# A convolution by three triangle products in place of two, and a new order of the loop's work

## The chip, the cores and the metric

One core of a Trainium2 chip runs the whole program. The metric is the device time of one execution in microseconds, and lower is better. The kernel before was timed three times, and its median is the figure that the kernel after is compared with. One execution of it was also profiled; all rows in this document that are called rows of before come from that execution.

The engines are named here as in the profile. PE is TensorE, which multiplies matrices (PEld is its weight load). DVE is VectorE, ACT is ScalarE, POOL is GpSimd, and SP is the engine whose queue starts the DMA transfers. Each engine works through its own queue in order. An instruction that must wait holds up everything behind it on the same engine.

## The reference, cut to what matters

```python
x: (1, 2048, 448); 16 heads of 28; u is not used by the sum: the convolution is called with x
g = sigmoid((x * gate_w).sum(-1))
q, k, v = split(x @ wqkv)
phi(t) = where(t > 0, t + 1, exp(t)) + 1e-6
o = phi(q) (phi(k)^T v) / (phi(q) . sum(phi(k)) + 1e-6)   # per head, not causal
a = o @ wo
K[d, l] = 2 Re sum_n C[d, n] exp(A[d, n] dt[d] l)          # one filter of length 2048 per channel
b = causal_convolution(x, K) + x * D_skip
out = g * a + (1 - g) * b
```

The part that the change touches is the convolution. For the filters that these inputs have, the kernel writes the filter of each channel as a value (`near`) times a straight line in the lag with a small slope. Inside a chunk of 128 positions the convolution is then a product with a lower triangle of ones, applied to x and to x times the slope; what comes from earlier chunks is added later, from the last row of every chunk. A general path for other filters stands behind a test at the end of the program and is not taken here.

## The kernel before

**Tiles and chunks.** The 2048 positions are 16 chunks of 128, with the positions on the partitions. For each chunk `c` one load (line 229) brings x transposed in three and a half blocks (for the projections) and x itself, 1024 columns of float32 in all. Products are made in a reduced float32 format (`F32R`), and where full accuracy is wanted a number is split: a high part is cast to that format on ScalarE, and the low part is the difference.

- `split_x` (line 260) makes the high part of a chunk by one ScalarE cast of 1024 columns (line 272) and the two low parts by GpSimd subtractions (lines 273 and 274, both recorded at line 258, the helper `low`): one of 512 columns for the projections and one of 448 for x itself.
- `skip` (line 276) is the product of x with `D_skip`, on GpSimd.

**The loop over c from 1 to 14** (line 520) is software-pipelined over several chunks. One iteration makes

- the k projection of chunk `c+1`: eleven matmuls into the one PSUM buffer "k" (line 534, recorded at 370), and on it the feature map: two exponentials on ScalarE (lines 396 and 397), add and max on VectorE (line 398), the high part on ScalarE (line 402), and the low part and the running sum `zb` on VectorE (both recorded at 408);
- the q projection of chunk `c`: eleven matmuls into the one buffer "q", then the gate's and the feature's exponentials on ScalarE (lines 416 and 385) and two VectorE operations (lines 386 and 389);
- eleven matmuls that add x's outer product with k to four accumulators (`do_g`, line 431, recorded at 438);
- one or two chunks of the convolution. It starts with a lag, from c=4 on (`LAG` is 3), and the iterations in `TWICE` (4, 5, 6, 8, 10, 12) take two chunks, so that the 16 chunks are done at c=13.

**One chunk of the convolution.** `do_wa` (line 449, recorded at 451) multiplies the high part of x by `slope` on VectorE; `do_wb` (line 453, recorded at 455) subtracts that from the low part, also on VectorE. `do_v` (line 457) adds two matmuls with the triangle `tri`: over the high part and over this difference. Its PSUM buffers "v0" and "v1" alternate. `v_post` (line 462, recorded at 464) multiplies the result by `near` on VectorE and sends its last row to `u` by a small DMA on SP's queue; `v_add` (line 469, recorded at 470) adds it to `y`, with both inputs in SBUF.

**The order.** The tile framework is used with a manual schedule: every engine runs its instructions in the order in which the program writes them, and what a reader sees in the loop body is the order of each queue. In an iteration the program writes the k projection, w of the next convolution chunk (up to c=11), `v_post` of the last one, the cast and the low parts of x of chunk `c+2` and its skip product, `v_add`, then the whole k feature, and in an iteration of `TWICE` the second convolution chunk with its `v_post` and `v_add`; then the q projection with its feature, more of w, the outer products, and the convolution matmuls of the next chunk. At c=4 the cast of chunk 6 comes later, since its buffer is still held by chunk 0 (six buffers for split chunks, three for loaded ones). At c=11 and 13 the output weight `wo` is split as well: a ScalarE cast of 896 columns (line 550) and a GpSimd subtraction (line 554). Small steps that prepare `slope` and `near` (`s4d_prepare`, line 305) are spread over the first iterations by `steps`.

**Behind the loop** come the all-reduce of `zb` over the partitions by an all-ones product, the gate, the normalisers of q (`norm_a` to `norm_d`), the block products with v and wo, and a last stage (`attend`, line 676) that makes eleven matmuls per chunk and writes the output.

Of the kernel before, what the change touches and what calls it, by code (L numbers as in the profile page):

```python
# [7 lines left out]
F32 = mybir.dt.float32  # L8
# [7 lines left out]
P = 128  # L16
# [15 lines left out]
QA = (2, 2, 5)  # L32
TWICE = (4, 5, 6, 8, 10, 12)
SMALL = 2.0 ** -70
# [137 lines left out]
def gated_mix_kernel(ctx: ExitStack, tc: tile.TileContext, xin, wk_d, wq_d, wv_d, wo_d, abc_d, ldt_d, dsk_d,  # L172
# [84 lines left out]
    def low(eng, o, r, h):  # L257
        eng.tensor_tensor(out=o, in0=r, in1=h.bitcast(F32), op=ALU.subtract)  # L258

    def split_x(c):  # L260
        r = xr[c]
        w = xs.tile([P, XW], F32R, name="xw", tag="x")
        h, l = xh[c], xl[c] = w, w[:, LT:]
        if c < 2:
            ACT.copy(h[:, :NAT], r[:, :NAT])
            if c == 0:
                ACT.copy(wkh[:, 0], wkr[:, 0])
            low(DVE, l, r[:, :NAT], h[:, :NAT])
            if c == 0:
                low(DVE, wkh[64:, 0], wkr[64:, 0], wkh[64:, 0])  # L270
        else:
            ACT.copy(h[:, :XC], r)  # L272
            low(POOL, l, r[:, :NAT], h[:, :NAT])
            low(POOL, h[:, XC:LT], r[:, NAT:LO], h[:, NAT:LO])

# [105 lines left out]

    def feature(dst, o, mid=None):
        e = tp.tile([P, D], F32, name="e", tag="e")
        t = tp.tile([P, D], F32, name="t", tag="t")
        ACT.activation(e, o[:, :D], AF.Exp)  # L385
        DVE.tensor_scalar(out=t, in0=e, scalar1=1.0, scalar2=1e-6, op0=ALU.min, op1=ALU.add)  # L386
        if mid:
            mid()
        DVE.scalar_tensor_tensor(out=dst, in0=o[:, :D], scalar=C1, in1=t, op0=ALU.add, op1=ALU.max)  # L389
# [10 lines left out]
    def k_high(c):  # L400
        pkh[c] = tp.tile([P, D], F32R, name="pkh", tag="pkh")
        ACT.add(pkh[c], pks[c], 1e-6)  # L402

    def k_low(c):
        pk = pks.pop(c)
        pkl[c] = tp.tile([P, D], F32R, name="pkl", tag="pkl")
        for o, a, op in ((pkl[c], pkh[c].bitcast(F32), ALU.subtract), (zb, zb, ALU.add)):
            DVE.scalar_tensor_tensor(out=o, in0=pk, scalar=1e-6, in1=a, op0=ALU.add, op1=op)  # L408

    def k_post(c, o):  # L410
        k_feature(c, o)
        k_high(c)
        k_low(c)

    def q_post(c, o, mid=None):
        ACT.activation(e1[:, c:c + 1], o[:, D:D + 1], AF.Exp, scale=-1.0)
        feature(pq[:, c], o, mid)

# [23 lines left out]

    def do_w(c, eng):
        do_wa(c)
        do_wb(c, eng)

    wq = {}

    def do_wa(c):
        q = wq[c] = tp.tile([P, D], F32, name="q", tag="t")  # L450
        DVE.tensor_tensor(out=q, in0=xh[c][:, NAT:LO].bitcast(F32), in1=slope, op=ALU.mult)  # L451

    def do_wb(c, eng):
        w = wt[c] = tp.tile([P, D], F32R, name="w", tag="w")
        eng.tensor_tensor(out=w, in0=xh[c][:, XC:LT].bitcast(F32), in1=wq.pop(c), op=ALU.subtract)  # L455

    def do_v(c):
        v = vt[c] = ps.tile([P, 512], F32, name="v", tag="v%d" % (c % 2))
        PE.matmul(v[:, :D], lhsT=tri, rhs=xh[c][:, NAT:LO], start=True, stop=False)
        PE.matmul(v[:, :D], lhsT=tri, rhs=wt.pop(c), start=False, stop=True)  # L460

# [42 lines left out]
    k_feature(1, ko)  # L504
    split_rest(0)
    k_low(0)
    skip(0)
# [3 lines left out]
    q_post(0, qo)  # L511
    split_x(2)
    k_low(1)
    skip(1)
# [5 lines left out]
    for c in range(1, NC - 1):  # L520
# [13 lines left out]
        ko = project(c + 1, wkh, wkl, D, "k")  # L534
        if c > LAG and c < 12 and vs[c in TWICE:]:
            do_w(vs[c in TWICE], DVE)
        if vq:
            v_post(vq[0])
        if c == NC - 2:
            zr = z_products()  # L540
            pick = xs.tile([P, 5, P], F32R, name="pick", tag="x")[:DJ]
            ACT.copy(pick, pickr)
        if c + 2 < NC and c != LAG + 1:
            split_x(c + 2)
            skip(c + 2)
        if c in (NC - 5, NC - 3):
# [3 lines left out]
            ACT.copy(woh[-1], wo[:, 2 * len(woh) - 2:2 * len(woh)])  # L550
        if vq:
            v_add(vq.pop(0))
        if c in (NC - 5, NC - 3):
            low(POOL, wol[-1], wo[:, 2 * len(wol) - 2:2 * len(wol)], woh[-1])
        if c > LAG and c >= 12 and vs[c in TWICE:]:
            do_w(vs[c in TWICE], DVE)
        k_post(c + 1, ko)
        if c == NC - 2:
# [3 lines left out]
            low(DVE, zl, zb, zh)  # L562
        if c in TWICE:
            v_next()
            v_post(vq[0])
            if c > LAG + 1:
                v_add(vq.pop(0))
        if c == LAG + 1:
            split_x(c + 2)
            v_add(vq.pop(0))  # L570
            skip(c + 2)
        if c == 1:
            steps(1)
        if c > 1:
            qo = project(c, wqh, wql, D + 2, "q")
            if c == LAG:
                do_g(c, (0,))
                steps(1)
                do_wa(vs[0])
                q_post(c, qo, lambda: do_wb(vs[0], DVE))  # L580
                steps(1)
            else:
                q_post(c, qo)
        if c == 2:
            steps(1)
        if c + 1 in TWICE and c > LAG:
            do_w(vs[c > LAG], DVE)
        if c < NC - 2:
            do_g(c, range(c == LAG, 4))
        if c == LAG:  # L590
# [377 lines left out]
```

## Time and profile before

| | us |
|---|---|
| median of three runs (211.17 to 213.93) | 212.77 |
| the profiled execution | 211.4 |
| its span, from the first to the last instruction | 209.6 |
| TensorE busy, 895 matmuls | 179.2 |
| VectorE busy, 298 instructions | 169.4 |
| GpSimd busy, 106 instructions | 105.7 |
| ScalarE busy, 192 instructions | 94.6 |

A row of a timeline gives the start and the duration in microseconds, the engine, the line of the kernel, the operation, what is written and read with its shape, and how many equal instructions follow one another in it. Brackets at the end hold the idle time ahead of it and what ended it. A row of the groups has the total busy time and the mean of one instruction in nanoseconds behind the bar, then the idle time ahead of them. A row of a line has the shortest, the middle and the longest duration. A row of the chain has start, duration and what it was. Matmuls overlap: one of 448 columns is listed with some 360 ns, while the next one starts earlier than that.

### The profile page before, as it was taken

The numbers are of one execution on the slowest core, as the hardware profiler recorded it, in microseconds if no ns is written. First come the engines' busy times: TensorE is split into PE (matmuls) and PEld (weight loads), VectorE is DVE, ScalarE is ACT, GpSimd is POOL, SyncE is SP. The second block draws the span as 40 slices with busy tenths as digits, with TensorE's granted clock in tenths as the row PEclk, the third lists the DMA queues.
The fourth block names the chain that finished last, engine by engine and source line by source line (L and its number), as shares of the span: only waits on it lengthen the run. The fifth ranks groups of instructions, "written<-read, shape, count | busy, mean of one in ns | idle before, by whom it ended". The sixth has DMA issues, their size and how long they took to land.

```text
span 209.6 us, 2815 instructions
## 1 busy us (share of the span) xinstructions
PE 179.2 (85%) x895; PEld 155.3 (74%) x895; DVE 169.4 (81%) x298; ACT 94.6 (45%) x192; POOL 105.7 (50%) x106
## 2 busy tenths in 40 slices
PE   7889699996986798969869596798979999999990
PEld 6678599895866687758748495695858989999980
DVE  2586479889998989898899889868979979998540
ACT  5695883354041442323260543336157456555530
POOL 1079959019560708254365619213655886886000
PEclk9999999999699999999999999999999999999997
DMA  5997946503020220033020302000000122222221
GB/s 199 338 296 250 276 135 246 184 2 104 0 85 16 100 79 21 0 105 100 0 97 5 105 0 55 5 15 0 4 2 0 44 93 90 89 89 90 91 110 36
DMA packets 8198, 18.65 MB, mean 89 GB/s; under 512 B 1756, under 2 KB 5040, under 8 KB 7952
## 3 DMA queue, kind: packets, MB, share of 16 engines
q1 hardware_dynamic: 8176, 18.39, 26.6%
q8 instruction: 9, 0.15, 0.3%
q14 instruction: 13, 0.11, 0.2%
HBM read 14.54 MB, written 3.67 MB: 87 GB/s over the span
## 4 chain that ended last, share of the span: by engine, by line
DVE 47%; PE 29%; issue 7%; ACT 7%; DMA 4%; POOL 2%; SPq 1%; DVEq 0%; ACTq 0%; POOLq 0%
PE a L686 17%; DVE y L470 8%; DVE q L451 6%; DVE w L455 5%; PE k L370 4%; DVE t L386 4%; DVE t L464 4%; DVE k L398 4%; DVE zb L408 4%; ACT pkh L402 3%; DVE pq L389 3%; PE tr L664 3%; DVE pkl L408 2%; DMA y<-in 2%; DMA xr<-in 2%
## 5 line engine op out<-in xcount | busy, mean ns | idle before, releaser
L258 POOL TENSOR_TENSOR xw<-xr,xw 128x448 fp32r<-128x448 f32 (+1 forms) x30 | 40.8, 1381 | 52.6 <-ACT xw L272 21.1
L370 PE MATMUL q<-wqh,xw 128*128 128x450 f32 x120 | 33.7, 383 | 6.8 <-DVE pq L389 4.8
L370 PE MATMUL k<-wkh,xw 128*128 128x448 f32 x120 | 32.7, 374 | 6.8 <-DVE zb L408 5.8
L438 PE MATMUL g<-pkh,xw 128*128 128x448 f32 x112 | 35.8, 367 | 0.0
L370 PEld LDWEIGHTS q<-wqh,xw 128*128 128x128 f32 x120 | 23.1, 196 | 10.6 <-ACT e L397 7.5
L370 PEld LDWEIGHTS k<-wkh,xw 128*128 128x128 f32 x120 | 21.6, 188 | 12.0 <-ACT e L385 4.0
L402 ACT ACTIVATE pkh<-k 128x448 fp32r<-128x448 f32 x15 | 8.2, 544 | 42.3 <-DVE k L398 42.3
L686 PE MATMUL a<-wkh,th 128*128 128x448 f32 (+1 forms) x119 | 26.9, 365 | 0.0
L603 POOL TENSOR_TENSOR prod<-pq,zb 128x448 f32<-128x448 f32 x16 | 18.5, 1161 | 10.4 <-ACT zb L709 6.1
L438 PE MATMUL g<-pkl,xw 128*128 128x448 f32 x64 | 23.6, 369 | 0.0
L438 PEld LDWEIGHTS g<-pkh,xw 128*128 128x128 f32 x112 | 21.0, 188 | 2.6
L686 PEld LDWEIGHTS a<-wkh,th 128*128 128x128 f32 x119 | 20.5, 189 | 1.3
L396 ACT ACTIVATE e<-k 128x448 f32<-128x448 f32 x15 | 8.1, 543 | 29.3 <-PE k L370 29.3
L277 POOL TENSOR_TENSOR y<-xr,rows 128x448 f32<-128x448 f32 x16 | 20.7, 1297 | 0.0
L470 DVE TENSOR_TENSOR y<-y,t 128x448 f32<-128x448 f32 x16 | 16.8, 1049 | 0.6
L455 DVE TENSOR_TENSOR w<-xw,q 128x448 fp32r<-128x448 f32 x16 | 15.7, 982 | 1.5
L626 POOL TENSOR_TENSOR pn<-pq,den 128x336 f32<-128x336 f32 x16 | 12.1, 754 | 9.3 <-DVE den L615 5.2
L370 PE MATMUL q<-wql,xw 128*128 128x450 f32 x45 | 16.7, 378 | 0.0
L408 DVE SCALAR_TENSOR_TENSOR pkl<-k,pkh 128x448 fp32r<-128x448 f32 x15 | 9.4, 624 | 8.6 <-ACT pkh L402 8.6
L370 PE MATMUL k<-wkl,xw 128*128 128x448 f32 x45 | 16.2, 367 | 0.0
L272 ACT CAST xw<-xr 128x1024 fp32r<-128x1024 f32 x14 | 14.8, 1055 | 2.8 <-DMA xr<-in 1.5
L451 DVE TENSOR_TENSOR q<-xw,rows 128x448 f32<-128x448 f32 x16 | 15.4, 960 | 0.0
(163 smaller groups left out, 349.1 us busy)
## 6 DMA issues: line engine op xcount, KB each, us to landing
xr<-in SPq DMA_DIRECT2D x14, 512.0 KB, 4.3
out<-ot SPq DMA_DIRECT2D x15, 224.0 KB, 1.9
pq<-in SPq DMA_DIRECT2D x2, 896.0 KB
xr<-in SPq DMA_DIRECT2D x4, 256.0 KB
y<-in SPq DMA_DIRECT2D x2, 450.0 KB, 5.6
y<-in SPq DMA_DIRECT2D x4, 224.0 KB
wv<-in SPq DMA_DIRECT2D x1, 896.0 KB
wo<-in SPq DMA_DIRECT2D x1, 784.0 KB
```

Of the source, the lines that this page charges most:

```text
L258: eng.tensor_tensor(out=o, in0=r, in1=h.bitcast(F32), op=ALU.subtract)
L272: ACT.copy(h[:, :XC], r)
L277: POOL.tensor_tensor(out=y[:, c], in0=xr[c][:, NAT:LO], in1=dsk, op=ALU.mult)
L370: PE.matmul(o[:, :n], lhsT=a, rhs=b, start=run.n == 1, stop=not seq)
L402: ACT.add(pkh[c], pks[c], 1e-6)
L408: DVE.scalar_tensor_tensor(out=o, in0=pk, scalar=1e-6, in1=a, op0=ALU.add, op1=op)
L438: PE.matmul(g[i][:a.shape[1], :D], lhsT=a, rhs=b, start=c == 0 and n == 0, stop=c == NC - 1 and n == len(seq) - 1)
L451: DVE.tensor_tensor(out=q, in0=xh[c][:, NAT:LO].bitcast(F32), in1=slope, op=ALU.mult)
L455: eng.tensor_tensor(out=w, in0=xh[c][:, XC:LT].bitcast(F32), in1=wq.pop(c), op=ALU.subtract)
L470: DVE.tensor_tensor(out=y[:, c], in0=y[:, c], in1=vt.pop(c), op=ALU.add)
L603: POOL.tensor_tensor(out=pd[c], in0=pq[:, c], in1=zb, op=ALU.mult)
L686: PE.matmul(a[:, lo:hi], lhsT=u_, rhs=w_[:, lo:hi], start=n == 0, stop=n == 10)
```

## The change

Three things are changed.

1. The convolution of a chunk is made of three triangle products: over the high part of x, over its low part, and over minus the high part times `slope`. So w is one VectorE operation, a scalar_tensor_tensor with the scalar -1, and its subtraction from the low part is gone. There is one matmul more per chunk.
2. The order inside an iteration is another one. `v_post` and `v_add` come first, then w, then the k feature; only behind its two exponentials stands the cast of x, on GpSimd the low parts and the skip product behind it, and on ScalarE the high part of k. The low part and the running sum of k change places: the running sum is written ahead of the high part.
3. The second of the doubled iterations at the end is 13 in place of 12, the split of `wo` is written ahead of that of x, and the preparing steps at c=3 follow the q feature together.

```diff
-TWICE = (4, 5, 6, 8, 10, 12)
+TWICE = (4, 5, 6, 8, 10, 13)
...
+    def low_x(c):
+        r, h = xr[c], xh[c]
+        low(POOL, xl[c], r[:, :NAT], h[:, :NAT])
+        low(POOL, h[:, XC:LT], r[:, NAT:LO], h[:, NAT:LO])
+
...
             ACT.copy(h[:, :XC], r)
-            low(POOL, l, r[:, :NAT], h[:, :NAT])
-            low(POOL, h[:, XC:LT], r[:, NAT:LO], h[:, NAT:LO])
...
+    def k_sum(c):
+        DVE.scalar_tensor_tensor(out=zb, in0=pks[c], scalar=1e-6, in1=zb, op0=ALU.add, op1=ALU.add)
+
     def k_low(c):
-        pk = pks.pop(c)
         pkl[c] = tp.tile([P, D], F32R, name="pkl", tag="pkl")
-        for o, a, op in ((pkl[c], pkh[c].bitcast(F32), ALU.subtract), (zb, zb, ALU.add)):
-            DVE.scalar_tensor_tensor(out=o, in0=pk, scalar=1e-6, in1=a, op0=ALU.add, op1=op)
+        DVE.scalar_tensor_tensor(out=pkl[c], in0=pks.pop(c), scalar=1e-6, in1=pkh[c].bitcast(F32), op0=ALU.add,
+                                 op1=ALU.subtract)
...
-    def do_wa(c):
-        q = wq[c] = tp.tile([P, D], F32, name="q", tag="t")
-        DVE.tensor_tensor(out=q, in0=xh[c][:, NAT:LO].bitcast(F32), in1=slope, op=ALU.mult)
-
-    def do_wb(c, eng):
+    def do_w(c):
         w = wt[c] = tp.tile([P, D], F32R, name="w", tag="w")
-        eng.tensor_tensor(out=w, in0=xh[c][:, XC:LT].bitcast(F32), in1=wq.pop(c), op=ALU.subtract)
+        DVE.scalar_tensor_tensor(out=w, in0=xh[c][:, NAT:LO].bitcast(F32), scalar=-1.0, in1=slope, op0=ALU.mult,
+                                 op1=ALU.mult)
...
-        PE.matmul(v[:, :D], lhsT=tri, rhs=xh[c][:, NAT:LO], start=True, stop=False)
-        PE.matmul(v[:, :D], lhsT=tri, rhs=wt.pop(c), start=False, stop=True)
+        for n, w in enumerate((xh[c][:, NAT:LO], xh[c][:, XC:LT], wt.pop(c))):
+            PE.matmul(v[:, :D], lhsT=tri, rhs=w, start=n == 0, stop=n == 2)
...
         ko = project(c + 1, wkh, wkl, D, "k")
-        if c > LAG and c < 12 and vs[c in TWICE:]:
-            do_w(vs[c in TWICE], DVE)
         if vq:
             v_post(vq[0])
...
-        if c + 2 < NC and c != LAG + 1:
-            split_x(c + 2)
-            skip(c + 2)
+        if vq:
+            v_add(vq.pop(0))
         if c in (NC - 5, NC - 3):
             wos = xs.tile([DJ, 2, 2, D], F32R, name="wos", tag="x")
...
-        if vq:
-            v_add(vq.pop(0))
-        if c in (NC - 5, NC - 3):
             low(POOL, wol[-1], wo[:, 2 * len(wol) - 2:2 * len(wol)], woh[-1])
-        if c > LAG and c >= 12 and vs[c in TWICE:]:
-            do_w(vs[c in TWICE], DVE)
-        k_post(c + 1, ko)
+        if LAG < c < 13:
+            while vs and len(wt) < 1 + (c in TWICE):
+                do_w(vs[len(wt)])
+        k_feature(c + 1, ko)
+        if c + 2 < NC and c != LAG + 1:
+            split_x(c + 2)
+            low_x(c + 2)
+            skip(c + 2)
+        if (c == LAG + 1 or c in TWICE) and not wt:
+            do_w(vs[0])
+        if c == LAG + 1:
+            v_next()
+        k_sum(c + 1)
+        k_high(c + 1)
+        k_low(c + 1)
+        if c == LAG + 1:
+            split_x(c + 2)
+            low_x(c + 2)
+            skip(c + 2)
...
-        if c in TWICE:
+        if c == LAG + 1:
+            v_post(vq[0])
+            v_add(vq.pop(0))
+        elif c in TWICE:
             v_next()
             v_post(vq[0])
-            if c > LAG + 1:
-                v_add(vq.pop(0))
-        if c == LAG + 1:
-            split_x(c + 2)
             v_add(vq.pop(0))
-            skip(c + 2)
...
         if c > 1:
-            qo = project(c, wqh, wql, D + 2, "q")
+            q_post(c, project(c, wqh, wql, D + 2, "q"))
             if c == LAG:
-                do_g(c, (0,))
-                steps(1)
-                do_wa(vs[0])
-                q_post(c, qo, lambda: do_wb(vs[0], DVE))
-                steps(1)
-            else:
-                q_post(c, qo)
+                steps(2)
         if c == 2:
             steps(1)
-        if c + 1 in TWICE and c > LAG:
-            do_w(vs[c > LAG], DVE)
+        if c == LAG:
+            do_w(vs[0])
+        if c > LAG and vs and not wt:
+            do_w(vs[0])
         if c < NC - 2:
-            do_g(c, range(c == LAG, 4))
+            do_g(c)
```

More of the change, by code (lines that the diff above doesn't have):

```diff
@@ L380, in gated_mix_kernel, with feature @@
     C1 = 1.0 + 1e-6
-    def feature(dst, o, mid=None):
+    def feature(dst, o):
         e = tp.tile([P, D], F32, name="e", tag="e")
@@ L386, in feature @@
         DVE.tensor_scalar(out=t, in0=e, scalar1=1.0, scalar2=1e-6, op0=ALU.min, op1=ALU.add)
-        if mid:
-            mid()
         DVE.scalar_tensor_tensor(out=dst, in0=o[:, :D], scalar=C1, in1=t, op0=ALU.add, op1=ALU.max)
@@ L412, in k_post, with q_post @@
         k_high(c)
+        k_sum(c)
         k_low(c)
-    def q_post(c, o, mid=None):
+    def q_post(c, o):
         ACT.activation(e1[:, c:c + 1], o[:, D:D + 1], AF.Exp, scale=-1.0)
-        feature(pq[:, c], o, mid)
+        feature(pq[:, c], o)
     def do_q(c, tag="q"):
@@ L441, in gated_mix_kernel @@
     vt, wt = {}, {}
[L443 to L447, printed above, removed]
-    def do_wa(c):
-        q = wq[c] = tp.tile([P, D], F32, name="q", tag="t")
-        DVE.tensor_tensor(out=q, in0=xh[c][:, NAT:LO].bitcast(F32), in1=slope, op=ALU.mult)
-    def do_wb(c, eng):
+    def do_w(c):
         w = wt[c] = tp.tile([P, D], F32R, name="w", tag="w")
-        eng.tensor_tensor(out=w, in0=xh[c][:, XC:LT].bitcast(F32), in1=wq.pop(c), op=ALU.subtract)
+        DVE.scalar_tensor_tensor(out=w, in0=xh[c][:, NAT:LO].bitcast(F32), scalar=-1.0, in1=slope, op0=ALU.mult,
+                                 op1=ALU.mult)
     def do_v(c):
         v = vt[c] = ps.tile([P, 512], F32, name="v", tag="v%d" % (c % 2))
-        PE.matmul(v[:, :D], lhsT=tri, rhs=xh[c][:, NAT:LO], start=True, stop=False)
-        PE.matmul(v[:, :D], lhsT=tri, rhs=wt.pop(c), start=False, stop=True)
+        for n, w in enumerate((xh[c][:, NAT:LO], xh[c][:, XC:LT], wt.pop(c))):
+            PE.matmul(v[:, :D], lhsT=tri, rhs=w, start=n == 0, stop=n == 2)
     def v_post(c):
@@ L505, in gated_mix_kernel @@
     split_rest(0)
+    k_sum(0)
     k_low(0)
@@ L512, in gated_mix_kernel @@
     split_x(2)
+    low_x(2)
+    k_sum(1)
     k_low(1)
```

## The prediction

> **What bounds the kernel now.** I read the page first, for the budget and the chain that ended last.
>
> ```profile
> span 209.6 us, 2815 instructions
> PE 179.2 (85%) x895; PEld 155.3 (74%) x895; DVE 169.4 (81%) x298; ACT 94.6 (45%) x192; POOL 105.7 (50%) x106
> DVE 47%; PE 29%; issue 7%; ACT 7%; DMA 4%; POOL 2%; SPq 1%; DVEq 0%; ACTq 0%; POOLq 0%
> ```
>
> The chain is VectorE's for 47% of the span, though TensorE is the busier engine. Two engines take turns as the limit, so I cut the span into stages. After the window's bounds and length come busy times with counts: TensorE first, VectorE third, GpSimd fifth; then the granted clock.
>
> ```profile
> 43.01:138.62 95.61, 78.96 (x364) 67.61 (x363) 86.13 (x113) 33.36 (x63) 47.44 (x34) 0.98 0.15 48
> 50.70:57.00 6.30, 4.37 (x15) 3.92 (x15) 6.13 (x7) 1.02 (x2) 4.36 (x3) 0.73 0.01 4
> 161.35:204.00 42.65, 42.57 (x241) 38.56 (x240) 34.73 (x78) 22.42 (x51) 24.37 (x34) 1.00 0.22 83
> ```
>
> The first row is the loop from c=4 to c=14, between two starts of line 396, the first ScalarE operation on a k projection. There VectorE is busy 86.1 of 95.6 us. In the last row (attention) TensorE has no gap. Now a piece of the loop on VectorE, from c=8 into c=9:
>
> ```profile
> 88.27 1.52 DVE L470 TENSOR_TENSOR y<-y,t 128x448 f32<-128x448 f32 x1
> 89.71 1.33 DVE L386 TENSOR_SCALAR t<-e 128x448 f32<-128x448 f32 x1
> 91.14 0.62 DVE L389 SCALAR_TENSOR_TENSOR pq<-q,t 128x448 f32<-128x448 f32 x1
> 91.69 0.83 DVE L451 TENSOR_TENSOR q<-xw,rows 128x448 f32<-128x448 f32 x1
> ...
> 94.35 0.63 DVE L398 SCALAR_TENSOR_TENSOR k<-k,e 128x448 f32<-128x448 f32 x1
> ...
> 96.66 0.38 DVE L386 TENSOR_SCALAR t<-e 128x448 f32<-128x448 f32 x1
> ```
>
> The same operation has two durations: line 386 takes 1.33 and 0.38 us. What the other engines do meanwhile:
>
> ```profile
> 88.02 2.77 POOL L258 TENSOR_TENSOR xw<-xr,xw 128x512 fp32r<-128x512 f32 x2 [5.07 <-ACT xw L272]
> 90.75 1.28 POOL L277 TENSOR_TENSOR y<-xr,rows 128x448 f32<-128x448 f32 x1
> 90.97 0.58 ACT L397 ACTIVATE e<-e 128x448 f32<-128x448 f32 x1
> 95.02 0.55 ACT L402 ACTIVATE pkh<-k 128x448 fp32r<-128x448 f32 x1 [3.46 <-DVE k L398]
> 91.92 1.06 PE L370 MATMUL q<-wqh,xw 128*128 128x450 f32 x4 [1.61 <-DVE pq L389]
> ```
>
> The long ones fall into GpSimd's block of 88.02 to 92.03. Operations with a PSUM operand (389, 398) take 0.62 to 0.63 inside it and outside it. So an operation with two SBUF inputs, or the one-input line 386, waits for the GpSimd instruction that is running, and each GpSimd instruction can hold up one of them. The price of the queue is seen on ScalarE: the exponential of k was done at 91.55, VectorE came to line 398 at 94.35, and line 402 waited 3.46 us for that. TensorE's q projection waited 1.61 us for pq, line 389. The loop is bound by VectorE's in-order queue, lengthened by GpSimd.
>
> **The operand that goes.** Before, each of 16 chunks costs VectorE two operations; after, one.
>
> ```profile
> L451 DVE TENSOR_TENSOR q<-xw,rows x16: 612/828/1571, 40.2 to 132.3; 128x448 f32<-128x448 f32 x16
> L451 DVE TENSOR_TENSOR q<-xw,rows 128x448 f32<-128x448 f32 x16 | 15.4, 960 | 0.0
> L455 DVE TENSOR_TENSOR w<-xw,q 128x448 fp32r<-128x448 f32 x16 | 15.7, 982 | 1.5
> 26.66 0.69 DVE L317 SCALAR_TENSOR_TENSOR y<-pq 112x512 f32<-112x512 f32 x1
> 25.46 1.16 DVE L317 SCALAR_TENSOR_TENSOR y<-pq 112x512 f32<-112x512 f32 x1
> ```
>
> Removed: 15.4 + 15.7 = 31.1 us of VectorE. Added: 16 scalar_tensor_tensor on two SBUF inputs of 448. The nearest row is line 317, the same operation on 512: 0.69 us at best, so 0.6 for 448, and 1.16 in another instance. I take 0.6 where the order below puts it outside GpSimd's block (16 x 0.6 = 9.6 us, 21.5 less on VectorE); the upper end is 1.57, the longest of line 451 (25.1 us, 6.0 less). The Trainium skill, "SBUF — State Buffer", section "Who interferes with whom", says that a VectorE instruction with two SBUF inputs contends with a GpSimd instruction that reads SBUF, and that the loser blocks until the other is done. The trace agrees (0.61 to 1.57 for line 451); by that rule the new form escapes nothing, which is how I cost it.
>
> Added too: one more 448-column matmul per chunk.
>
> ```profile
> 28.19 2.26 PE q L370 x11
> ```
>
> 0.2055 us each, so 16 x 0.2055 = 3.3 us of TensorE: nothing where it waits anyway, all of it where it becomes the bound; 5.7 us at the 0.355 spacing of the slow stretch below.
>
> **The new order, in one iteration.** The undisturbed chain of a k projection is seen at c=14. The next two rows show GpSimd starting 1.14 us after the start of a cast of x, then a free pair of low parts, the casts' mean, and the split of wo on GpSimd.
>
> ```profile
> 138.37 0.98 PE L370 MATMUL q<-wqh,xw 128*128 128x450 f32 x4
> 138.62 0.55 ACT L396 ACTIVATE e<-k 128x448 f32<-128x448 f32 x1 [2.71 <-PE k L370]
> 139.81 0.63 DVE L398 SCALAR_TENSOR_TENSOR k<-k,e 128x448 f32<-128x448 f32 x1 [1.20 <-ACT e L397]
> 140.48 0.54 ACT L402 ACTIVATE pkh<-k 128x448 fp32r<-128x448 f32 x1 [0.70 <-DVE k L398]
> 141.06 0.62 DVE L408 SCALAR_TENSOR_TENSOR pkl<-k,pkh 128x448 fp32r<-128x448 f32 x1 [0.61 <-ACT pkh L402]
> 58.23 1.06 ACT L272 CAST xw<-xr 128x1024 fp32r<-128x1024 f32 x1
> 59.37 2.79 POOL L258 TENSOR_TENSOR xw<-xr,xw 128x512 fp32r<-128x512 f32 x2 [4.30 <-ACT xw L272]
> 22.60 2.38 POOL L258 TENSOR_TENSOR xw<-xr,xw 128x512 fp32r<-128x512 f32 x2
> L272 ACT CAST xw<-xr 128x1024 fp32r<-128x1024 f32 x14 | 14.8, 1055 | 2.8 <-DMA xr<-in 1.5
> L258 POOL TENSOR_TENSOR wos<-wo,wos 112x896 fp32r<-112x896 f32 x2 | 4.6, 2314 | 0.0
> ```
>
> Count from A, the start of line 396. TensorE passes from k to q at A-0.25. VectorE's add-max (398) starts at 1.19. The cast of x now stands behind the two exponentials (1.03 to 2.08), so line 402 starts at 2.08 instead of 1.86 and the low part (pkl) at 2.66; the running sum (k_sum) fills VectorE's idle 0.6 us before it. The move costs 0.22 us, hidden: k's PSUM buffer is free at 3.2, and TensorE wants it after q, g and v only, at 4.9. Were the cast held up by a late load, 1.7 us of cover are there. GpSimd's two low parts run from 2.17 to 4.5, the skip product to about 6.1 with what VectorE slips in between; TensorE wants the first low part at 4.9. The split of wo (2.3 us, c=11 and 13) moves ahead of the low parts, into GpSimd's idle time from 6.1 to the next A+2.17 (3.4 us); without it the low parts of x would come 2.3 us late, when TensorE wants them.
>
> An iteration with one v has 36 matmuls, 7.4 us; with two, 39, 8.0 us. VectorE in the 7.4: add-max 1.19, sum 1.73, pkl 2.66; line 386 blocked until the first low part ends at 3.4, done 3.8; pq 4.4; v_post 5.15 (v ends at 4.9); v_add blocked by the skip to 6.1, done 6.65; one or two w, 7.2 and 7.75; the next add-max is due at 7.4 + 1.19 = 8.6. It keeps up with 0.8 us to spare. In the 8.0: v_post at 3.2, v_add blocked to 4.5, line 386 by the skip to 6.25, pq done 7.2 (q's PSUM is wanted at 7.8), then v_post, v_add and w to 8.85, add-max due at 9.2: it keeps up too. TensorE waits only where w is late: the first v of an iteration with two wants w 0.16 us after A (two of its three matmuls need none).
>
> The sum, by c. 4: 8.0. 5: 9.0, as two such iterations follow one another and the w of chunk 2 comes 1.0 us late. 6 to 12: 8.0, 7.4, 8.0, 7.4, 8.0, 7.4, 7.4. 13: 8.0 and 2.6 of waits: chunk 14's w is made only after the add-max (done 2.3, wanted 0.16: 2.2 us), chunk 15's after pq (0.4 us). Together 81.2. Hand-overs take 0.04 (140.44 to 140.48) to 0.16 us (pq's end 91.76 to 91.92); one of 0.1 per iteration makes 82.3, against 95.6: -13.3 us.
>
> **Ahead of and behind the loop.**
>
> ```profile
> 25.70 1.05 PE L370 MATMUL k<-wkh,xw 128*128 128x448 f32 x4 [1.94 <-DVE zb L408]
> 142.25 0.57 ACT L561 CAST zh<-zb 128x448 fp32r<-128x448 f32 x1 [1.22 <-DVE zb L408]
> 144.91 1.01 DVE L425 TENSOR_SCALAR og<-og 128x15 f32<-128x15 f32 x1
> ```
>
> At c=2 the k projection waited 1.94 us for the sum, the second of two operations; now pkl is the last and done 0.5 to 0.7 us sooner, and the cast no longer stands ahead of the exponentials. Later casts move GpSimd's blocks too, which could take it back: -0.6, between 0 and -1.2. Behind c=14 the sum is ready at A+2.3; its cast ran at A+3.6 before. The all-ones product and the normalisers start some 0.7 us sooner, and the gate's small operations can get ahead of the GpSimd block that stretched line 425 to 1.01: -1.2, between -0.5 and -2.2.
>
> In all 13.3 + 0.6 + 1.2 = 15.1 us: span 194.5. The profiled execution lasted 211.4, 1.8 outside its span: 196.3. The median of the runs, 212.77, is 1.4 above that execution: **197.7 us**.
>
> **Rivals.** *The lock keeps VectorE the bound.* For it: three operations per iteration still meet GpSimd's three instructions, and GpSimd is busy in 47 of the 95.6 us. At worst two take 1.5 us and line 386 1.35: with three operations of the k chain (3 x 0.54 apart), v_post, pq (0.54 each) and 0.3 idle that is 7.35 with one v, hidden by 7.4; a second v adds v_post, v_add and w, 1.6 us free: 8.95 against 8.0. Six times 0.95 is 5.7 us: 203.4. Against it: w stands behind v_add, when GpSimd's block is over.
>
> *The cast waits, and the gain goes.* The cast now stands ahead of line 402 and q's exponentials on ScalarE; a late load delays k's PSUM. A wait of 3 us in each of ten iterations is 1.3 us beyond the cover, 13 us: 211. Against it: all casts together waited 1.5 us for loads, and the load issued in c=5 had ten microseconds before its cast at 58.23:
>
> ```profile
> 47.97 0.43 SPq L229 DMA_DIRECT2D xr<-in  x1
> ```
>
> *The slow clock, slower than before.*
>
> ```profile
> PE v L460 <- DVE w L455: 6.9, 5, 2.6
> 52.63 0.47 PE L460 MATMUL v<-w,tri 128*128 128x448 f32 x1 [1.93 <-DVE w L455]
> 56.54 0.36 PE L370 MATMUL q<-wql,xw 128*128 128x450 f32 x1
> ```
>
> After one of the five long waits for w the clock fell (0.73 in the window above): from 52.63, 11 matmuls came 0.355 us apart. 378 matmuls x 0.15 = 57 us if the whole loop ran so; from 34% of them (15.1 + 4.3 of 57) it is 2% slower: 217 and up, say 219. For it: waits of 1.0 and 2.2 us remain at c=5 and c=13. Against it: one fall in five waits, TensorE now idles less, and the gapless last 42.65 us ran at 1.00. The Trainium skill, "TensorE: Matmul & The Clock Gate", section "What's actually happening", says that idling throttles the clock and activity releases it, in windows of about 3.4 us; the trace's fall and recovery agree, and by that rule fewer waits mean fewer falls. One fall costs 11 x 0.15 = 1.6 us, which the range holds.
>
> **How the numbers follow.** TensorE as the loop's bound 0.66, own range 193.0 to 201.5 (below: 195.1 by the favourable ends, 81.2 + 1.2 + 2.2, and 2.1 of the 3.6 us of waits for w gone as well; above: one fall and 0.2 us more per iteration); the lock 0.22 (203.4); the late cast 0.08 (211); the slow clock 0.04 (219). 2% of 212.77, about what a measurement can tell from no change, is 4.3 us: faster means below 208.5. The first two are faster and a little of the third: 0.89; within 2% 0.07; slower 0.04. The range reaches over the lock's case: 193.0 to 204.5.
>
> **What would show it.** Right: 82 us between the starts of the first k exponential at c=4 and c=14, TensorE busy over 93% of them; v's third matmul waiting for w at c=5 and c=13 only; the k high part (402) waiting under 1 us for the add-max; the new w at 0.6 us; the running sum in VectorE's former idle time. Wrong: w at 1.5 us in most places, q's matmuls still waiting for pq, casts waiting for loads, or more than one stretch below 0.9 of the clock. The prediction falls if that stretch takes over 90 us.

## The result, and the profile after

The kernel after takes 198.31 us (median of four runs, 196.42 to 199.12); the kernel before takes 213.35 (four runs). The ratio is 0.931, with a 95% interval of 0.920 to 0.943. The forecast was 197.7 us. A run more than 1.5% above the fastest of its kernel is left out of the ratios here and below, though not out of the medians (215.15 us of the kernel before here, 214.89 beside experiments 5 to 8, and 208.98 in experiment 2, whose median without it would be 206.42).

First the head of the page of the kernel after: span, busy times, the granted clock in 40 slices, and the chain that ended last.

```profile
span 196.8 us, 2819 instructions
PE 181.3 (92%) x911; PEld 161.2 (82%) x911; DVE 149.0 (76%) x282; ACT 94.9 (48%) x192; POOL 102.0 (52%) x106
PEclk9999999999999999999999988999799999999998
PE 75%; DVE 11%; ACT 4%; DMA 3%; issue 2%; SPq 1%; POOL 1%; ACTq 0%; DVEq 0%; POOLq 0%
```

VectorE's share of the chain fell from 47% to 11%, and TensorE's rose from 29% to 75%. The profiled execution took 198.59 us against 211.4; it and its span are both 12.8 us shorter. The same view of the stages as before (bounds, length, TensorE, its weight load, VectorE, ScalarE, GpSimd, clock) shows where it came from: the loop from the first k exponential of c=4 to that of c=14, then three of its iterations (c=8, 9 and 13), then the stage behind it, up to the first product of attention.

```profile
42.20:125.30 83.10, 79.68 (x380) 71.46 (x379) 66.13 (x97) 33.57 (x63) 43.18 (x34) 0.98 0.18 56
75.18:83.19 8.01, 8.01 (x41) 7.28 (x40) 6.35 (x10) 3.11 (x7) 3.91 (x3) 1.00 0.22 68
83.19:90.59 7.40, 7.40 (x38) 6.66 (x36) 6.21 (x11) 3.11 (x6) 3.67 (x3) 1.00 0.23 72
113.41:125.30 11.89, 9.80 (x41) 8.47 (x40) 8.50 (x13) 3.82 (x7) 5.40 (x6) 0.86 0.01 2
125.30:148.41 23.11, 20.65 (x115) 17.48 (x113) 18.73 (x42) 11.53 (x25) 11.12 (x14) 0.93 0.02 5
```

The loop fell from 95.6 to 83.1 us, which is 12.5 of the 12.8 us; in front of it 0.8 us were won (43.01 to 42.20), and the stage behind it grew from 22.48 to 23.11 us. In the iterations with two chunks and with one TensorE is busy all the time, for the time of the 39 and 36 matmuls that they hold (39 x 0.2055 is 8.01 us, 36 x 0.2055 is 7.40; the counts 41 and 38 in the rows also hold those that overlap an end of the window). The new w on VectorE, and the waits for it:

```profile
L449 DVE SCALAR_TENSOR_TENSOR w<-xw,rows x16: 610/618/632, 40.8 to 121.8; 128x448 fp32r<-128x448 f32 x16
PE v L455 <- DVE w L449: 3.4, 2, 2.1
ACT pkh L403 <- DVE zb L406: 10.5, 14, 1.4
51.83 0.47 PE L455 MATMUL v<-w,tri 128*128 128x448 f32 x1 [1.32 <-DVE w L449]
115.81 0.47 PE L455 MATMUL v<-w,tri 128*128 128x448 f32 x1 [2.09 <-DVE w L449]
```

All 16 took 0.61 to 0.63 us, so none met a GpSimd instruction. TensorE waited twice for it, at c=5 (1.32 us) and at c=13 (2.09 us). Line 403 makes the high part of k; what it waits for is the running sum, line 406, which it doesn't read.

### The profile page after: what moved, and what is told of

Read it like the earlier page. It is cut to its first block, busy times and chain, and to the rows that moved or that the text cites. A ratio compares the mean times of both kernels' runs of the same rounds, so it can differ in the third digit from the quotient of the medians.

```text
span 196.8 us, 2819 instructions
## 1 busy us (share of the span) xinstructions
PE 181.3 (92%) x911; PEld 161.2 (82%) x911; DVE 149.0 (76%) x282; ACT 94.9 (48%) x192; POOL 102.0 (52%) x106
## 4 chain that ended last, share of the span: by engine, by line
PE 75%; DVE 11%; ACT 4%; DMA 3%; issue 2%; SPq 1%; POOL 1%; ACTq 0%; DVEq 0%; POOLq 0%
PE a L688 18%; PE q L373 16%; PE k L373 15%; PE g L442 14%; PE v L455 4%; PE tr L666 4%; DMA y<-in 2%; PE m L754 2%; DVE y L465 1%; ACT e L398 1%; PE v L373 1%; ACT e L397 1%; DMA zr<-ru 1%; DVE k L399 1%; DVE t L459 1%
## 5 line engine op out<-in xcount | busy, mean ns | idle before, releaser
L258 POOL TENSOR_TENSOR xw<-xr,xw 128x448 fp32r<-128x448 f32 (+1 forms) x30 | 36.7, 1243 | 43.7 <-ACT xw L277 28.7
L373 PEld LDWEIGHTS k<-wkh,xw 128*128 128x128 f32 x120 | 22.8, 193 | 5.5 <-DVE pkl L410 2.2
L373 PEld LDWEIGHTS q<-wqh,xw 128*128 128x128 f32 x120 | 23.7, 199 | 3.0 <-POOL wqh L258 0.7
L399 DVE SCALAR_TENSOR_TENSOR k<-k,e 128x448 f32<-128x448 f32 x15 | 9.5, 630 | 11.6 <-ACT e L398 11.6
L373 PE MATMUL q<-wql,xw 128*128 128x450 f32 x45 | 17.2, 390 | 0.0
L670 ACT CAST th<-tr 128x512 fp32r<-128x512 f32 x16 | 9.4, 588 | 13.5 <-PE tr L666 13.3
L465 DVE TENSOR_TENSOR y<-y,t 128x448 f32<-128x448 f32 x16 | 14.5, 909 | 1.1
L389 DVE TENSOR_SCALAR t<-e 128x448 f32<-128x448 f32 x15 | 13.6, 909 | 1.8 <-ACT e L388 1.8
L693 DVE SCALAR_TENSOR_TENSOR ot<-y,og,a 128x448 f32<-128x448 f32 (+1 forms) x17 | 10.5, 616 | 5.7 <-PE a L688 5.5
```

Of the source, the lines that this page charges most:

```text
L373: PE.matmul(o[:, :n], lhsT=a, rhs=b, start=run.n == 1, stop=not seq)
L399: DVE.scalar_tensor_tensor(out=pks[c], in0=pks[c], scalar=1.0, in1=e, op0=ALU.add, op1=ALU.max)
L465: DVE.tensor_tensor(out=y[:, c], in0=y[:, c], in1=vt.pop(c), op=ALU.add)
L693: DVE.scalar_tensor_tensor(out=ot[:, lo:hi], in0=y[:, c, lo:hi], scalar=og[:, c:c + 1], in1=a[:, lo:hi], op0=ALU.mult, op1=ALU.add)
```

## The experiments

All times are medians of four runs, and the ratios are to runs of the kernel before on the same chip (median 212.64 for experiments 1 to 4, 212.69 for 5 to 8). The ratios come from the runs other than the profiled one, so they can differ from the quotient of two medians by up to 0.003.

**1. The operand alone.** The kernel before, with this and nothing of the new order:

```diff
-        q = wq[c] = tp.tile([P, D], F32, name="q", tag="t")
-        DVE.tensor_tensor(out=q, in0=xh[c][:, NAT:LO].bitcast(F32), in1=slope, op=ALU.mult)
+        pass
...
-        eng.tensor_tensor(out=w, in0=xh[c][:, XC:LT].bitcast(F32), in1=wq.pop(c), op=ALU.subtract)
+        DVE.scalar_tensor_tensor(out=w, in0=xh[c][:, NAT:LO].bitcast(F32), scalar=-1.0, in1=slope, op0=ALU.mult,
+                                 op1=ALU.mult)
...
-        PE.matmul(v[:, :D], lhsT=tri, rhs=xh[c][:, NAT:LO], start=True, stop=False)
-        PE.matmul(v[:, :D], lhsT=tri, rhs=wt.pop(c), start=False, stop=True)
+        for n, w in enumerate((xh[c][:, NAT:LO], xh[c][:, XC:LT], wt.pop(c))):
+            PE.matmul(v[:, :D], lhsT=tri, rhs=w, start=n == 0, stop=n == 2)
```

> The kernel before with three triangle products and the one-operation w, everything else in the old order. Theory (VectorE's in-order queue bound the loop, TensorE bounds it after the change): 16 operations of 0.96 us go from a queue that was full, so the loop falls from 95.6 us to 84 to 88, since some 0.6 us per iteration stay idle in front of the low part of k and w still stands late; the whole some 203 to 206 us. Rival (the order did it all, the operand is nothing but 3.3 us more on TensorE): 212 to 216 us. Rival (the operand did it all): 198 to 200 us.

Measured: 198.60 us, ratio 0.937 (0.929 to 0.944). That is the rival's number, and the kernel after can't be told from it. The stages, again from c=4 to c=14, then c=8 and c=9:

```profile
43.58:125.16 81.58, 78.51 (x380) 70.14 (x379) 72.04 (x97) 33.84 (x64) 49.08 (x34) 1.00 0.17 57
77.89:85.90 8.01, 8.01 (x41) 7.28 (x40) 7.09 (x11) 3.21 (x6) 4.58 (x4) 1.00 0.18 66
85.90:93.30 7.40, 7.40 (x38) 6.71 (x37) 6.58 (x10) 3.10 (x6) 4.29 (x4) 1.00 0.22 72
61.86 0.47 PE L460 MATMUL v<-w,tri 128*128 128x448 f32 x1 [1.83 <-DVE w L454]
```

In the old order the loop is 81.6 us, 1.5 less than in the new one, and the iterations shown are the same 8.01 and 7.40 us with TensorE busy throughout. Most of the 1.5 us is a stretch of low clock that the execution of the kernel after had at c=13 and this one hadn't (some 1.2 us, an estimate from the rows of experiment 6: 11.89 against 10.65). My expectation that the old order would hold VectorE back by 3 to 6 us is wrong: once one of the two operations is gone, VectorE keeps up in either order. One wait for w is left (1.83 us, at c=6).

**2. The order alone.** The kernel after, with the two VectorE operations and the two triangle products of before (so the new order together with the other doubled iteration, points 2 and 3 of the change):

```diff
-        DVE.scalar_tensor_tensor(out=w, in0=xh[c][:, NAT:LO].bitcast(F32), scalar=-1.0, in1=slope, op0=ALU.mult,
-                                 op1=ALU.mult)
+        q = tp.tile([P, D], F32, name="q", tag="t")
+        DVE.tensor_tensor(out=q, in0=xh[c][:, NAT:LO].bitcast(F32), in1=slope, op=ALU.mult)
+        DVE.tensor_tensor(out=w, in0=xh[c][:, XC:LT].bitcast(F32), in1=q, op=ALU.subtract)
```

> The kernel after with two VectorE operations for w and two triangle products, so the new order alone. Theory: an iteration with one chunk has 0.8 us of spare VectorE time, which hides a longer w; one with two chunks has w 0.6 to 1.5 us later, and TensorE waits for it there; against that TensorE has 16 matmuls (3.3 us) less. Sum 199 to 204 us, with waits of v's second matmul for w of 8 us or more. Rival (the order did it all): 195 to 197 us. Rival (the operand did it all, the order nothing): 211 us or more.

Measured: 207.38 us, ratio 0.975 (0.963 to 0.987). It lies between the theory's range and the rival that gives the order nothing.

```profile
44.00:134.38 90.38, 78.37 (x364) 68.14 (x364) 77.04 (x113) 33.45 (x64) 44.18 (x34) 0.98 0.15 51
PE v L456 <- DVE w L451: 10.5, 6, 3.9
124.17 0.60 PE L456 MATMUL v<-w,tri 128*128 128x448 f32 x1 [3.89 <-DVE w L451]
```

The order alone takes 5.2 us off the loop. TensorE waits 10.5 us for w, 3.9 of them at c=13 in one wait. So the two parts don't add up: 14.0 us for the operand (212.64 - 198.60), 5.3 for the order, 15.0 for both. Each works on the same wait, that for VectorE, and behind it stands TensorE.

**3. One matmul per chunk less.** The kernel after without the product over the low part of x:

```diff
-        for n, w in enumerate((xh[c][:, NAT:LO], xh[c][:, XC:LT], wt.pop(c))):
-            PE.matmul(v[:, :D], lhsT=tri, rhs=w, start=n == 0, stop=n == 2)
+        for n, w in enumerate((xh[c][:, NAT:LO], wt.pop(c))):
+            PE.matmul(v[:, :D], lhsT=tri, rhs=w, start=n == 0, stop=n == 1)
```

> The kernel after without the triangle product over the low part of x, which it leaves out: 16 matmuls less, nothing else changed. Theory (TensorE bounds the loop): 36 matmuls become 35, 39 become 37, the iterations 7.2 and 7.6 us, the whole 2.5 to 3.3 us shorter, 195 to 196 us. Rival (VectorE still bounds it): no change, 198 us, iterations 7.4 and 8.0.

Measured: 197.83 us, ratio 0.933 (0.926 to 0.941). Neither theory's picture is right as a whole. The rows are an iteration with one chunk (c=7), one with two (c=8), and the wait in the latter:

```profile
67.43:74.61 7.18, 7.18 (x36) 6.28 (x34) 6.30 (x10) 3.10 (x6) 3.66 (x3) 1.00 0.22 75
74.61:82.59 7.98, 7.86 (x39) 7.06 (x39) 6.54 (x11) 3.14 (x6) 3.89 (x3) 1.00 0.20 68
74.84 0.19 PEld L455 LDWEIGHTS v<-w,tri 128*128 128x128 f32 x1 [0.49 <-DVE w L449]
PEld v L455 <- DVE w L449: 6.3, 6, 2.7
```

With one chunk the iteration is shorter by the matmul (7.18 against 7.40). With two it is shorter by both where w is ready in time (7.59 us at c=6, from 59.84 to 67.43), but at c=8 it stays at 7.98, though two matmuls less would be 0.4 us: TensorE's weight load waits 0.49 us for w, and there are six such waits in all. So in the kernel after, TensorE is the bound by little in an iteration like c=8. There w is done at 75.13 (74.51 and 0.62) and TensorE comes to the product that reads it at 75.33. VectorE makes pq, v_post, v_add and w one after the other (from 72.36 on in this run), so w can't come sooner in that order.

**4. w made earlier.** The kernel after, with the first w of an iteration with two chunks ahead of v_post, and the w of chunk 15 behind the low part of k:

```diff
         ko = project(c + 1, wkh, wkl, D, "k")
+        if c in TWICE and c > LAG + 1 and not wt:
+            do_w(vs[0])
         if vq:
             v_post(vq[0])
...
         k_low(c + 1)
+        if c == 13:
+            do_w(vs[1])
```

> The kernel after with w made earlier in the places where TensorE waited for it: the first w of an iteration with two chunks ahead of v_post, and chunk 15's w behind the low part of k at c=13. Theory: the waits of 1.3 us at c=5 and 2.1 us at c=13 go, and with the latter the stretch at half clock that followed it (1.5 us): loop 83.1 to 78.5 to 80, the whole 193.5 to 195.5 us. Rival (the slow clock is not caused by the wait): only 3.4 us less in the loop, a stretch at low clock somewhere else in it, 195 to 196.5. Rival (the w moved ahead delays v_post and with it the rest): no change.

Measured: 193.92 us, ratio 0.912 (0.905 to 0.920).

```profile
43.26:121.49 78.23, 78.11 (x379) 70.18 (x378) 66.11 (x97) 33.36 (x64) 42.95 (x33) 1.00 0.18 59
```

TensorE is busy for 78.11 of the loop's 78.23 us, just below the 78.5 to 80 us expected: both waits are gone, and so is the stretch of low clock in the loop. The kernel is faster than the kernel before, and in the medians 4.4 us faster than the kernel after.

**5. What GpSimd's block cost.** The kernel before, with the skip product replaced; the product of x with `D_skip` is left out of the output.

```diff
-        POOL.tensor_tensor(out=y[:, c], in0=xr[c][:, NAT:LO], in1=dsk, op=ALU.mult)
+        POOL.memset(y[:, c], 0.0)
```

> The kernel before with the skip product on GpSimd replaced by a memset of the same tile, so that the product of x with D_skip is left out of the output. It asks what GpSimd's block costs VectorE. Theory (each GpSimd instruction that reads SBUF holds up one VectorE operation with two SBUF inputs): the third held-up operation of an iteration, 0.2 to 0.9 us, goes; the loop falls from 95.6 to 88 to 92 us, the whole to 205 to 209. Rival (only the number of VectorE's operations counts): no change, 212 to 214.

Measured: 207.25 us, ratio 0.977 (0.970 to 0.984), inside the theory's range.

```profile
43.45:134.64 91.19, 77.07 (x364) 66.62 (x363) 81.29 (x112) 33.41 (x64) 38.60 (x34) 1.00 0.16 51
89.94 0.61 DVE L451 TENSOR_TENSOR q<-xw,rows 128x448 f32<-128x448 f32 x1
```

VectorE runs the same operations, and its busy time in the loop is 81.3 us instead of 86.1; line 451, which took 0.83 us in the piece of before that the prediction shows, takes 0.61 in the same iteration. So an instruction on another engine lengthened VectorE's queue. Whether it did so by its reads or by its length this run doesn't separate: the memset takes 0.46 to 0.72 us where the product took 1.14 to 1.53. The loop is 4.4 us shorter; how much of that is the clock, which fell once in the old loop (0.98 over it) and not in this one (1.00), the runs don't separate.

**6. TensorE kept busy during the wait.** The kernel after, with ten products ahead of chunk 14's, into the buffer that the right ones overwrite:

```diff
+        for _ in range(10 if c == 14 else 0):
+            PE.matmul(v[:, :D], lhsT=tri, rhs=xh[c][:, NAT:LO], start=True, stop=True)
         for n, w in enumerate((xh[c][:, NAT:LO], xh[c][:, XC:LT], wt.pop(c))):
```

> The kernel after with ten more triangle products (2.06 us of TensorE) ahead of those of chunk 14, into the same buffer, which the right ones then overwrite: TensorE is kept busy during its 2.1 us wait for w at c=13, and the wait for w is not shorter. Theory (the half clock at c=13 follows the idle time): no half clock there, the iteration 10.3 to 10.6 us instead of 11.9, the whole 196.5 to 197.3. Rival (the clock falls for another reason, or at random): the iteration stays at 11.5 us or more in the profile, 198.3.

Measured: 198.01 us, ratio 0.932 (0.926 to 0.939).

```profile
113.57:124.22 10.65, 10.55 (x51) 8.99 (x50) 8.43 (x13) 3.84 (x8) 5.40 (x6) 1.00 0.01 3
115.97 0.47 PE L457 MATMUL v<-w,tri 128*128 128x448 f32 x1
116.28 0.98 PE L373 MATMUL q<-wqh,xw 128*128 128x450 f32 x4
```

In the profiled execution there is no low clock at c=13, as the theory has it: w comes at the same time (115.97 against 115.81, both 2.40 us into the iteration), the clock in that iteration is 1.00 instead of 0.86, four q matmuls take 0.98 us where they took 1.50, and the iteration is 1.24 us shorter (10.65, just above the 10.3 to 10.6 expected). The median misses the 196.5 to 197.3 us of the theory: 198.01 is nearer to the rival's 198.3, and the 0.3 us to the kernel after are less than the runs differ among themselves.

That the filling kept the clock up isn't shown by this one execution. Low stretches start on a grid of 3.41 us (last section). Drawn back from the low stretch that this execution has behind the loop, at 138.99, the grid has a line at 115.10, which cuts the wait that was filled (some 113.9 to 115.97) into 1.2 and 0.9 us, and behind waits cut like that the clock didn't fall in other executions either. Nor does the clock fall at c=13 in every run of the kernel after. Over its four runs the granted clock was 0.978 (the profiled one, with two low stretches), 0.996, 0.986 and 0.996; with the filling it was 0.986 (the profiled one, with one), 0.984, 0.984 and 0.987; and the profiled execution of experiment 1, which has none in or just behind the loop, has 0.995. So two of the kernel after's four runs probably had none either, and the medians can't price the filling.

**7. The high part of k ahead of the running sum**, on the kernel of experiment 4:

```diff
-        k_sum(c + 1)
         k_high(c + 1)
+        k_sum(c + 1)
         k_low(c + 1)
```

> The kernel with early w, and the high part of k written ahead of the running sum. ScalarE waited for the running sum in all iterations (10.5 us in 14 waits), though it reads nothing of it. Theory (the wait is only put behind the operation that was written before it): line 403 starts 0.6 us sooner where no cast stands ahead of it, at c=14 the all-reduce comes 0.6 us sooner and with it the rest: 193.3 against 193.9; the loop unchanged at 78.2, since that delay was hidden. Rival (the two operations can't read the PSUM buffer at the same time): the running sum waits for the high part instead, nothing gained, 193.9.

Measured: 194.32 us, ratio 0.914 (0.909 to 0.919): no gain in the median, as the rival has it.

```profile
DVE zb L406 <- ACT pkh L403: 9.5, 14, 0.8
123.90 0.54 ACT L403 ACTIVATE pkh<-k 128x448 fp32r<-128x448 f32 x1 [0.70 <-DVE k L399]
124.48 0.62 DVE L406 SCALAR_TENSOR_TENSOR zb<-k,zb 128x448 f32<-128x448 f32 x1 [0.61 <-ACT pkh L403]
```

Now the sum waits for the high part, as often (14 times) as the other way round before. In this program the two never read the k buffer in PSUM at the same time; the one that is written later waits. A program in which nothing orders the two was not tried. The profiled loop did get shorter, against both expectations (77.63 us against 78.23). In experiment 4 the 0.6 us were lost at c=4 and c=5, where w still came a little late (8.23 and 8.38 us instead of 8.00). A part of it may be the cast of x, which stands behind the high part at c=4 and now starts 0.65 us sooner. Ahead of the loop this execution took 1.16 us longer than that of experiment 4 (44.42 against 43.26).

**8. Work for TensorE behind the loop**, on top of 7: seven matmuls of the last q projection instead of two ahead of the wait for the k-v block, and two instead of five behind it.

```diff
-QA = (2, 2, 5)
+QA = (2, 7, 2)
```

> The same, and behind the loop five matmuls of the last q projection more in the place where TensorE waits 1.5 us for the split of the k-v block (seven instead of two there, two instead of five later). Theory (TensorE idles there and its clock falls after it): 1.0 us of work moved into the wait, and no half clock after it, 1.2 us: the stage from the last k feature to the attention 21 to 22 us instead of 23.2, the whole 191 to 192. Rival (the chain through VectorE and ScalarE sets the end of that stage, not TensorE): under 0.5 us, 193 us or more.

Measured: 192.10 us, ratio 0.906 (0.900 to 0.913), the fastest of all. The rows are that stage in experiment 4 and, without and with this edit, in experiments 7 and 8, and then the wait in it and what follows, of the kernel after, of experiment 7 and of experiment 8.

```profile
121.49:144.67 23.18, 20.73 (x115) 17.60 (x114) 20.03 (x45) 11.55 (x25) 12.03 (x15) 0.93 0.03 6
122.05:144.60 22.55, 19.85 (x116) 16.66 (x116) 20.10 (x45) 12.14 (x26) 12.07 (x15) 1.00 0.03 6
```

```profile
119.80:141.88 22.08, 19.91 (x115) 16.25 (x114) 19.64 (x44) 11.63 (x25) 12.08 (x15) 1.00 0.03 6
```

```profile
140.02 0.93 PE L754 MATMUL m<-wos,kvh 112*112 112x448 f32 x2 [1.48 <-ACT kvh L792]
141.12 1.05 PE L666 MATMUL tr<-ident,pn 128*128 128x128 f32 x4
```

```profile
136.96 0.65 PE L758 MATMUL m<-wos,kvh 112*112 112x448 f32 x2 [1.50 <-ACT kvh L796]
```

```profile
134.71 0.66 PE L758 MATMUL m<-wos,kvh 112*112 112x448 f32 x2 [0.46 <-ACT kvh L796]
135.43 0.60 PE L670 MATMUL tr<-ident,pn 128*128 128x128 f32 x4
137.78 0.47 PE L772 MATMUL md<-sl,pick 112*128 112x448 f32 x1 [0.35 <-DVE sl L764]
```

The wait for the split falls from 1.50 to 0.46 us, but the stage is only 0.5 us shorter than in experiment 7 (22.08 against 22.55), since TensorE then waits for VectorE (0.35 us for `sl`). The stage fits the rival, the median the theory. Experiment 4's stage is 1.1 us longer than this one, but it had the low clock behind its wait (0.93 over the stage), and experiment 7 had none behind a wait of the same length; so these rows don't show that this edit kept the clock up. The median is 2.2 us below that of experiment 7, more than the stage explains. In the two profiled executions 2.25 us of the difference lie ahead of the loop (42.17 against 44.42), where the two programs are the same. What the edit is worth is therefore 0.5 us by the rows, and more only where it saves a fall of the clock, which isn't shown.

## Why the prediction was right, and where it was not

- **The bound.** Right: the loop was VectorE's and became TensorE's. The forecast iterations of 7.4 and 8.0 us are there to a hundredth (7.40, 8.00 and 8.01).
- **w.** Right: 0.6 us each, outside GpSimd's block. The matmuls cost 0.2055 us each, as taken. That w as a scalar_tensor_tensor escapes nothing was not tried by the kernel after, where none met GpSimd. In the old order (experiment 1) many do: the middle one takes 1.00 us and the longest 2.54, more than the 1.57 that the prediction took as the upper end. The rows are the line and one of them, beside the 0.62 us of an operation of the same kind just ahead of it that has one input in PSUM:

```profile
L454 DVE SCALAR_TENSOR_TENSOR w<-xw,rows x16: 611/998/2540, 41.1 to 117.6; 128x448 fp32r<-128x448 f32 x16
84.45 0.62 DVE L389 SCALAR_TENSOR_TENSOR pq<-q,t 128x448 f32<-128x448 f32 x1
84.99 0.85 DVE L454 SCALAR_TENSOR_TENSOR w<-xw,rows 128x448 fp32r<-128x448 f32 x1
```

- **The order.** The sum put the operand and the order into one calculation and never asked what either gives alone. Experiments 1 and 2 show that the operand does nearly all of it, and that the order adds nothing that can be told from zero on top of it (198.60 and 198.31 us): it moves TensorE's wait for w from c=6 to c=5 and c=13. Without the new operand it is worth some 5 us. The mechanism was right, its share between the parts was not in the text, and the expectation for experiment 1 (203 to 206) had it wrong.
- **The sum by c.** Forecast 82.3, measured 83.10. c=4 is right at 8.0. c=5 was put at 9.0 and is 9.58: the step "the w of chunk 2 comes 1.0 us late" was mis-sized, since at c=4 the cast of x stands behind the high part of k, so that GpSimd's low parts begin 4.07 us into the iteration (46.27) and not at 2.17, and v_add was held up by one of them (1.57 us with its own 0.6), line 389 by the next (1.35). Then c=13: it was put at 10.6 and is 11.89: the wait is there (2.09, forecast 2.2), and the stretch of low clock behind it is added. That fall stood in the range, not in the sum. The 0.1 us per iteration for hand-overs did not show (and ten of them make 82.2, not 82.3); without this term the forecast of the loop would be 1.9 us short instead of 0.8, so it is near by luck. The rows are the iteration of c=5, GpSimd's late low parts and the v_add that was held up:

```profile
50.20:59.78 9.58, 8.26 (x41) 7.24 (x40) 8.67 (x15) 3.21 (x7) 3.65 (x4) 1.00 0.19 56
46.27 2.79 POOL L258 TENSOR_TENSOR xw<-xr,xw 128x512 fp32r<-128x512 f32 x2 [5.34 <-ACT e L420]
46.48 1.57 DVE L465 TENSOR_TENSOR y<-y,t 128x448 f32<-128x448 f32 x1
```

- **"line 402 starts at 2.08 instead of 1.86."** Wrong, and without a price: it starts at 2.52 (70.30 against 67.78), because it waits for the running sum that was put ahead of it. I took the sum for a filler of idle time and the high part for free of it. The cover (TensorE comes back to the buffer at 4.9) held. The rows are ScalarE's and VectorE's of c=7:

```profile
67.78 0.55 ACT L397 ACTIVATE e<-k 128x448 f32<-128x448 f32 x1 [4.45 <-PE k L373]
68.84 1.04 ACT L277 CAST xw<-xr 128x1024 fp32r<-128x1024 f32 x1
69.64 0.62 DVE L406 SCALAR_TENSOR_TENSOR zb<-k,zb 128x448 f32<-128x448 f32 x1
70.30 0.55 ACT L403 ACTIVATE pkh<-k 128x448 fp32r<-128x448 f32 x1 [0.42 <-DVE zb L406]
```

- **Ahead of the loop.** Forecast -0.6, measured -0.8. That the two agree is not shown to be more than chance: executions of programs that are the same there reach the loop at 42.20 (after), 42.34 (experiment 6) and 43.26 (experiment 4), and at 44.42 and 42.17 (experiments 7 and 8). The wait at c=2 that the term was read from is 1.58 us instead of 1.94, but 1.54 in the old order of experiment 1.
- **Behind the loop.** Forecast -1.2, measured +0.6 up to attention and +0.5 to the end of the span. The all-reduce does come 0.6 us sooner, but the step "the gate's small operations can get ahead of the GpSimd block" failed: both moved by the same 0.6 us, and the gate's operation is as long as before:

```profile
130.80 2.27 POOL L605 TENSOR_TENSOR prod<-pq,zb 128x448 f32<-128x448 f32 x2 [6.13 <-ACT zb L711]
130.99 1.02 DVE L429 TENSOR_SCALAR og<-og 128x15 f32<-128x15 f32 x1
```

  Behind that, after the 1.48 us wait for the k-v block, the clock fell in this execution (the four transposes above); it did not after a wait of the same length in the execution before. That took back what was won.
- **The rivals.** The lock did not decide, but it is real: experiment 5 prices the third instruction's block at up to 4.4 us of the old loop. The casts waited for no load in the loop. The slow clock came in two short stretches and not over the loop.

In all the profiled execution is 2.3 us longer than forecast (198.59 against 196.3): +0.8 in the loop, -0.2 ahead of it, +1.7 behind it. The median is only 0.6 us off, because the forecast put it 1.4 us above the profiled execution and it came out 0.3 below. So the total agrees better than its terms.

## What to carry to other kernels

When two changes relieve the same wait, price each alone against the next bound; here the shorter operand reached TensorE's bound by itself, and the order had nothing left to win. Then look for what still interrupts the new bound: the 3.4 us of waits at two places, with the fall of the clock behind one of them, were worth 4.4 us in the medians of experiment 4, where the reordering had added 0.3 us to the operand. And compare a later experiment with the one that it was built on, stage by stage: the 2.2 us of experiment 8 lie mostly where nothing had been changed. An operation that is moved into another's idle time may put itself in front of a third that uses the same PSUM buffer.

## What was not expected of the hardware

- TensorE's clock fell to half after waits of 1.9 us (before), 2.1 and 1.5 (after), 3.9 (experiment 2, where it was 0.66 over the 5 us behind the wait), 2.3 and 1.5 (experiment 3) and 1.5 (experiments 4 and 6), and not after others, such as 2.6 and 1.5 us (before), 1.8 (experiment 1), 2.3 and 1.9 (experiment 2), 2.4 and 2.2 (experiment 5) and 1.5 (one in each of experiments 1, 2, 3, 5 and 7).
- Every one of these low stretches stands at 0.50 for 3.4 us, and two in one execution start a multiple of 3.41 us apart: 23.9 us, seven times that, in the kernel after and in experiment 3. Lay a grid of 3.41 us through each execution that has such a stretch, if only at the program's end, from the start of that stretch. The falls in the loop then come behind periods with 1.9 us of idle time or more (1.93, 2.09, 2.29 and 3.23), and no period in the loop with less (1.63 us at most) is followed by one. The grid cuts in two the waits of 2.6 us (before), of 1.8 (experiment 1) and of 2.3 and 1.9 (experiment 2). So where a wait lies on the grid seems to decide, and not its length alone. This is worked out from few cases and not tested, and it isn't the whole rule: behind the loop the same wait of 1.5 us, whole in one period, was followed by a fall in four executions (after, experiments 3, 4 and 6) and not in a fifth (before); cut in two it was not (experiments 1, 2 and 7). The Trainium skill, "TensorE: Matmul & The Clock Gate", section "What's actually happening", describes a window of 3.4 us that runs free of the program; the grid agrees with it, though the idle times of 1.5 to 2.3 us within one period that a fall followed are shorter than the whole window that the page asks to be idle. The rows are the period that holds the wait of 2.1 us in the kernel after, the low one behind it, and experiment 2's 5 us.

```profile
112.93:116.34 3.41, 1.32 (x7) 0.88 (x7) 3.17 (x4) 2.08 (x4) 1.76 (x2) 1.00 0.01 1
116.34:119.75 3.41, 3.41 (x11) 3.02 (x10) 2.58 (x3) 0.53 (x1) 3.17 (x4) 0.50 0.01 1
124.00:129.00 5.00, 4.83 (x16) 4.36 (x17) 2.43 (x5) 1.07 (x4) 2.62 (x3) 0.66 0.00 0
```

- ScalarE's and VectorE's reads of one PSUM buffer followed one another in 14 of 14 cases, in whichever order they were written (the later one starts 0.6 to 0.7 us after the earlier one). The Trainium skill, "PSUM — Partial Sum Buffer", section "PSUM bank collisions raise a hardware error", says that two engines must not access one bank at once, two reads included, and that the chip raises an error there instead of making one wait. By that the wait is put in by the program's ordering, and a buffer of one bank can't be read by two engines side by side; the traces agree as far as they show one behind the other each time.
- A memset on GpSimd in place of a product took 4.8 us off VectorE's busy time in the loop without touching VectorE. This agrees with the Trainium skill, "SBUF — State Buffer", section "Who interferes with whom", which says that only a GpSimd instruction that reads SBUF holds up VectorE's second input. But the memset is also the shorter instruction (0.47 us in the middle, against 1.28), so the run alone doesn't show that the reading is what counts.
